# First Y of a delta-rule and MoE kernel placed by products, and the unpacking steps of ScalarE and VectorE given out anew

## The chip, the cores and the metric

One core of a Trainium2 chip runs the whole kernel. The metric is the device time of one execution in microseconds, the median over runs. Engines are called PE (TensorE), PEld (its weight loads), ACT (ScalarE), DVE (VectorE), POOL (GpSimd) and SP (SyncE, which here only starts transfers).

## The reference

```python
# batch 4, 8 heads, 768 steps, head size 48; w_in 384 x 2048, w_out 2048 x 384
for t in range(S):
    y[:, :, t] = einsum('bhd,bhde->bhe', q_t, state)
    v_old = einsum('bhde,bhd->bhe', state, k_t)          # k normalised
    state = state + beta_t * einsum('bhd,bhe->bhde', k_t, v_t - v_old)
x = y.transpose(0, 2, 1, 3).reshape(3072, 384)
h = x @ w_in
g = where(h >= 1, h, where(h <= -1, 0, (h + 1)**2 / 4))
out = g @ w_out
```

## The kernel before

The 768 steps are cut into 12 chunks of 64, and two chunks make a pair G = 0 to 5. A chunk goes through a chain: `gram_k`, `gram_q` (products of keys with keys, and of queries with keys), a triangular solve on DVE in steps of 16-blocks (L312 multiply, L314 subtract), merges of the solved blocks on PE (`merge16_a`, `merge16_b`, `merge32`), `chain_r` and `chain_u` (rows of the state's update, copied from PSUM into the tile SU), `chain_y` (the chunk's Y) and `chain_d` (the new state). `scale_v` and the masks L235 prepare the next operands on DVE, with work of ACT.

Y of a pair is written to XB, in two parts: a rounded one (hi, ACT) and the rest (lo, DVE, L479), so that full-precision products can be made from three fast ones. XB wants the 384 model columns in three groups of 128 rows. A head has 48 columns and a bank row 64, so of every four heads three stand where they belong with the gap between them filled by the fourth, cut in three parts of 16. In all chunks that fourth quarter is first put in a staging tile (`stg`, L477 for its lo part) and then moved by six transfers that SP starts (L482). 

The MoE part runs in items, one weight tile of 128 columns (`f`, 16 of them) and a pair's tokens each. `up` makes nine products (L638), then ACT clamps twice (L777) and squares (L804), DVE takes the maximum (L806), `rest` splits the result into `ghi` (ACT, L772) and `glo` (DVE, L773), and two items later `down` (LAG = 2) adds it into four output banks (L653). The first pair, G = 0, has 22 items: tiles 0 to 5 with the first chunk's tokens only, then tiles 6 to 15 with both chunks', then tiles 0 to 5 with the second chunk's. It is only here that weight tiles are unpacked, each in five steps: grow (ACT, L179), shift (DVE, L181), join (DVE, L183), cast to the hi part (ACT, L187), and low, the lo part (DVE, L189). Four buffers (X4, `xb`) hold tiles in work. Tiles wt11 to wt15 get their weights late, and their rooms serve as scratch before.

Order: the kernel is written under a manual schedule, so every engine works in the order in which the code issues its instructions. `stage` runs the pieces of the front, the part ahead of item 0: products on PE, some steps of ACT and DVE, then their evictions (`finish`). In the items, `at(pe, G, t, ...)` and `at(fill, G, t, ...)` hang pieces on half items: t = 2.5 is the second half of item 2. Before, the generator `unpack` fixed which steps of which tiles go together, as in the following lines, and it was advanced at three places in an item.

```python
        for f in range(2, FT):
            step(f + 1)
            step(f)
            yield
            step(f)
            step(f)
            yield
            step(f - 1)
            yield
```

The idle products, L586 (`IDLE` = 34 of them), stand in the front while the first solve runs on DVE. Chunk names in the text: the first pair holds chunks 0 and 1, the second pair 2 and 3.

Of the kernel before, what the change touches and what calls it, by code (L numbers as in the profile page):

```python
# [27 lines left out]


@with_exitstack  # L30
def delta_rule_moe(ctx: ExitStack, tc: tile.TileContext, kqa, kqb, kv, beta, w, out):
# [142 lines left out]
    def weight(f):  # L174

        x = X4[:, f % 4]
        st = RAW.pop(f)
        sti, xi = st.bitcast(I32), x.bitcast(I32)
        nc.scalar.activation(out=x, in_=st[:, :, 1::2], func=AF.Prelu, scale=2.0 ** -112, alpha=2.0 ** 32)  # L179
        yield  # L180
        nc.vector.tensor_scalar(out=xi, in0=xi, scalar1=3, scalar2=None, op0=ALU.logical_shift_left)  # L181
        yield
        nc.vector.scalar_tensor_tensor(out=xi, in0=sti[:, :, 0::2], scalar=29, in1=xi, op0=ALU.logical_shift_right, op1=ALU.bitwise_or)  # L183
        yield
# [1 line left out]
        hi, lo = (WT[f][:, :, i, :] for i in range(2))
        nc.scalar.copy(out=hi, in_=x)  # L187
        yield
        nc.vector.tensor_tensor(out=lo, in0=x, in1=hi, op=ALU.subtract)  # L189
        yield  # L190
# [231 lines left out]
    def chain_u(g):  # L422
        b_ = banks(D)
        for j in range(H):
            for e, o in quarters():
# [2 lines left out]
                nc.tensor.matmul(b_[t][o * C:o * C + C, j], XT[r, g % 2, k, :], KV[g][r, 1, k, :], start=True, stop=True)  # L428

        def evict():  # L430
            for o in range(2):
                nc.scalar.copy(out=SU[o * C:o * C + C, o, 0:H], in_=b_[1][o * C:o * C + C])  # L432
            nc.scalar.copy(out=SU[:, 0, H:NU], in_=b_[0])
        return evict

    def chain_y(g):
# [10 lines left out]
        def product(i, e, p, o, x, rows, **how):  # L447
            k = e * H + i * NP + p
            u = (x * NU + k) * D
            nc.tensor.matmul(yy[i][o * C:o * C + C, e, p], SF[rows, u:u + C], w_[rows, x, k, :], **how)  # L450
# [79 lines left out]
    def unpack():  # L530

        gens = [weight(f) for f in range(FT)]

        def step(f):
            if f < FT:
                next(gens[f])
        step(0)
        step(1)
        step(0)
        yield  # L540
        step(0)
        step(0)
        yield
        step(2)
        step(1)
        yield
        step(0)
        yield
        step(1)
        step(1)  # L550
        yield
        for f in range(2, FT):
            step(f + 1)
            step(f)
            yield
            step(f)
            step(f)
            yield
            step(f - 1)
            yield  # L560
        step(FT - 1)
        yield

    def stage(pieces, *fill):
# [36 lines left out]
    run(ln[1], 2)
    stage(one_(merge16_b, 0))
    run(ln[1])
    early = solve(), unlanes(1)
    stage(one_(merge32, 0, None, True), (early[0], 4))
    weight_loads(4, 5, nc.scalar)
    stage(one_(merge32, None, 0), (sv[0], 2), (early[0], 4))
    stage(both(chain_u, 0), (raws[0][1], 9), (wu, 2))
    weight_loads(5, 6, nc.scalar)
    stage(both(chain_y, 0), (wu, 2))  # L610
    weight_loads(6, 7)
    stage(both(chain_d, 0), (wu, 2))
    stage(one_(merge16_a, 1), (wu, 2))
# [75 lines left out]
    def plan(G):  # L689

        a, b = 2 * G + 2, 2 * G + 3
        if G == NS - 1:
            return
        va, vb = scale_v(a), scale_v(b)
        if G == 0:
            for j, f in ((0, merge16_b), (0.5, chain_r), (1, lambda g: merge32(g, None, True)), (2, lambda g: merge32(None, g)), (3, chain_u), (4, chain_y), (5, chain_d)):
                at(pe, G, j, lambda f=f: f(1))
            back = restore()
            at(fill, G, 0, (sv[1], 2))
            at(fill, G, 1, (load_k, b), (weight_loads, 7, 9), (load_q, a), (weight_loads, 9, 10), (load_kv, a), (weight_loads, 10, 13))  # L700
            at(fill, G, 1.5, (back, 1))
            at(fill, G, 2.5, (back, 1), (raws[1][1], 9))
            for j, n in enumerate((2, 2, 3)):
                at(fill, G, 3.5 + j, (early[0], n))
            at(fill, G, 6.5, (early[1], 1))
            at(fill, G, 7, (early[1], 9))
            at(fill, G, 4.5, (load_q, b), (weight_loads, 13, 14))
            at(fill, G, 5.5, (load_kv, b), (weight_loads, 14, 15))
            at(fill, G, 8, (load_k, a + 2), (weight_loads, 15, FT))
            for j in range(2):  # L710
                at(fill, G, 6 + j / 2, (va, 1))
                at(fill, G, 11.5 + j / 2, (vb, 1))
            at(pe, G, 6, lambda: gram_q(a))
            at(pe, G, 7, lambda: chain_r(a))
            at(pe, G, 11, lambda: gram_q(b))
            for j, f in ((8, merge16_a), (9.5, merge16_b)):
                for g in range(2):
                    at(pe, G, j + g / 2, lambda f=f, g=g: f(g))
# [60 lines left out]
    late, last, ready = [], None, []  # L779
    for n, item in enumerate(items):  # L780
        at_, c = 2 * n, cols(item[2])
        finish(late)
# [21 lines left out]
        nc.scalar.activation(out=s[:, c], in_=s[:, c], func=AF.Square)  # L804
# [1 line left out]
        nc.vector.tensor_tensor(out=s[:, c], in0=h[:, c], in1=s[:, c], op=ALU.max)  # L806
# [56 lines left out]
```

## Time and profile before

| what | us |
|---|---|
| median of three runs (lowest, highest) | 621.3 (621.08, 621.97) |
| the profiled execution | 622.07 |
| its span, from first to last instruction | 620.2 |
| PE busy | 584.1 (94%) |
| DVE busy | 395.6 (64%) |
| ACT busy | 393.7 (63%) |
| POOL busy | 29.8 (5%) |

The page cuts the span into 40 slices of 15.5 us; each digit is the busy share of a slice in tenths, and PEclk the clock granted to PE, in tenths of full speed:

```profile
PE   8956978799999999999999999999999999999997
...
DVE  5986579783369882469983389963489954323332
ACT  3436676559666659575568647578646576566664
...
PEclk8556597899999999999999999999999999999999
```

The first nine slices, up to 140 us, hold the front and the first pair's items with a weight tile to unpack: there PE has gaps and a lower clock. After it PE is 90% busy or more in each slice to the last.

### The profile page before, as it was taken

The numbers are of one execution on the slowest core, as the hardware profiler recorded it, in microseconds if no ns is written. First come the engines' busy times: TensorE is split into PE (matmuls) and PEld (weight loads), VectorE is DVE, ScalarE is ACT, GpSimd is POOL, SyncE is SP. The second block draws the span as 40 slices with busy tenths as digits, with TensorE's granted clock in tenths as the row PEclk, the third lists the DMA queues.
The fourth block names the chain that finished last, engine by engine and source line by source line (L and its number), as shares of the span: only waits on it lengthen the run. The fifth ranks groups of instructions, "written<-read, shape, count | busy, mean of one in ns | idle before, by whom it ended". The sixth has DMA issues, their size and how long they took to land.

```text
span 620.2 us, 21724 instructions
## 1 busy us (share of the span) xinstructions
PE 584.1 (94%) x9562; PEld 513.4 (83%) x9562; DVE 395.6 (64%) x832; ACT 393.7 (63%) x685; POOL 29.8 (5%) x62
## 2 busy tenths in 40 slices
PE   8956978799999999999999999999999999999997
PEld 7855866687889888888888888888888888889986
DVE  5986579783369882469983389963489954323332
ACT  3436676559666659575568647578646576566664
POOL 5110000010001000010000020000020000000000
PEclk8556597899999999999999999999999999999999
DMA  5663665400124300215210214210225000020001
GB/s 139 196 199 118 199 217 158 144 3 4 42 61 108 83 21 14 53 31 130 82 30 4 71 39 121 65 30 12 61 62 131 4 3 15 8 59 1 0 1 51
DMA packets 32830, 42.96 MB, mean 69 GB/s; under 512 B 7152, under 2 KB 27440, under 8 KB 32736
## 3 DMA queue, kind: packets, MB, share of 16 engines
q1 hardware_dynamic: 31360, 39.14, 22.5%
q10 hardware_dynamic: 1120, 2.36, 1.1%
q8 instruction: 75, 1.23, 0.8%
q14 instruction: 19, 0.16, 0.1%
q0 software_dynamic: 256, 0.08, 0.1%
HBM read 34.47 MB, written 4.72 MB: 63 GB/s over the span
## 4 chain that ended last, share of the span: by engine, by line
PE 68%; ACT 15%; DVE 7%; SPq 4%; DMA 3%; issue 3%; ACTq 0%; DVEq 0%
PE o L653 27%; PE h L638 26%; PE ch L450 3%; ACT s L777 2%; ACT GG L402 2%; ACT XT L404 2%; PE ch L412 2%; SPq L482 2%; DVE xb L183 2%; PE ch L428 1%; PE ch L221 1%; PE ch L494 1%; ACT s L804 1%; ACT XT L397 1%; ACT ghi L772 1%
## 5 line engine op out<-in xcount | busy, mean ns | idle before, releaser
L638 PE MATMUL h<-xb,wt 128*128 128x512 f32 (+1 forms) x918 | 229.5, 396 | 8.0 <-DMA xb<-wt 7.4
L653 PE MATMUL o<-wt,ghi 128*128 128x384 f32 x768 | 202.8, 346 | 0.0
L638 PEld LDWEIGHTS h<-xb,wt 128*128 128x128 f32 x918 | 167.7, 196 | 41.0 <-ACT xb L179 3.9
L806 DVE TENSOR_TENSOR s<-h,s 128x512 f32<-128x512 f32 (+1 forms) x102 | 66.8, 655 | 132.5 <-ACT s L804 132.3
L653 PEld LDWEIGHTS o<-wt,ghi 128*128 128x128 f32 x768 | 138.8, 190 | 7.0
L653 PE MATMUL o<-wt,glo 128*128 128x384 f32 x384 | 130.6, 340 | 0.0
L772 ACT CAST ghi<-s 128x512 fp32r<-128x512 f32 (+1 forms) x102 | 60.8, 596 | 92.2 <-DVE s L806 74.1
L777 ACT ACTIVATE s<-h,half 128x512 f32<-128x512 f32 (+1 forms) x102 | 67.5, 662 | 40.0 <-PE h L638 39.1
L773 DVE TENSOR_TENSOR glo<-s,ghi 128x512 fp32r<-128x512 f32 (+1 forms) x102 | 66.7, 654 | 39.5 <-ACT ghi L772 39.2
L653 PEld LDWEIGHTS o<-wt,glo 128*128 128x128 f32 x384 | 73.0, 190 | 0.2 <-DVE glo L773 0.2
L777 ACT ACTIVATE s<-s,one 128x512 f32<-128x512 f32 (+1 forms) x102 | 71.6, 702 | 2.2
L804 ACT ACTIVATE s<-s 128x512 f32<-128x512 f32 (+1 forms) x102 | 61.9, 607 | 3.2
L323 DVE TENSOR_TENSOR pr<-A 128x30 f32<-128x30 f32 (+14 forms) x120 | 39.3, 328 | 6.2 <-POOL A L294 4.5
L325 DVE TENSOR_TENSOR A<-A,pr 128x30 f32<-128x30 f32 (+14 forms) x120 | 39.9, 332 | 4.4
L187 ACT CAST wt<-xb 128x768 fp32r<-128x768 f32 x16 | 13.3, 832 | 32.0 <-DVE xb L183 32.0
L450 PEld LDWEIGHTS ch<-Q,SU 64*64 64x64 f32 (+1 forms) x1008 | 22.1, 135 | 4.3 <-ACT ghi L772 1.5
L450 PE MATMUL ch<-Q,SU 64*64 64x64 f32 (+1 forms) x1008 | 24.3, 222 | 0.7 <-ACT SU L432 0.7
L235 DVE TENSOR_TENSOR Q<-ch,mask 64x512 f32<-64x512 f32 (+1 forms) x30 | 20.6, 688 | 0.4
L294 POOL TENSOR_SCALAR_AFFINE_SELECT A<-A 128x1024 f32<-128x1024 f32 x4 | 5.1, 1263 | 314.2 <-DMA xb<-X 259.1
L402 ACT ACTIVATE GG<-ch 32x512 f32<-32x512 f32 x22 | 12.9, 588 | 9.8 <-PE ch L390 9.5
L509 DVE TENSOR_TENSOR SU<-ch,SU 48x384 f32<-48x384 f32 (+1 forms) x29 | 16.1, 555 | 0.4
L390 PEld LDWEIGHTS ch<-XT,GG 32*32 32x32 f32 x704 | 13.1, 110 | 3.7 <-issue 3.0
(150 smaller groups left out, 607.2 us busy)
## 6 DMA issues: line engine op xcount, KB each, us to landing
wt<-in_w_dram SPq DMA_DIRECT2D x14, 768.0 KB, 4.9
out_dram<-wx SPq DMA_DIRECT2D x44, 96.0 KB, 2.2
KV<-in_kv_dram SPq DMA_DIRECT2D x36, 96.0 KB, 2.5
KV<-in_kv_dram SPq DMA_DIRECT2D x72, 48.0 KB, 2.4
KV<-in_kv_dram SPq DMA_DIRECT2D x12, 192.0 KB, 2.7
xb<-X SPq DMA_DIRECT2D x60, 32.0 KB, 2.0
K<-in_kqb_dram SPq DMA_DIRECT2D x12, 128.0 KB, 2.7
Q<-in_kqb_dram SPq DMA_DIRECT2D x12, 128.0 KB, 2.8
```

Of the source, the lines that this page charges most:

```text
L235: nc.vector.tensor_tensor(out=a, in0=a if copied else b, in1=mask[r, None, :].broadcast_to([r.stop - r.start, H, C]), op=ALU.mult)
L323: nc.vector.tensor_tensor(out=pr, in0=A[:, 0:n, j:j + 1].broadcast_to([P, n, m]), in1=A[:, j:j + 1, j + 1:32].broadcast_to([P, n, m]), op= ...
L325: nc.vector.tensor_tensor(out=A[:, 0:n, j + 1:32], in0=A[:, 0:n, j + 1:32], in1=pr, op=ALU.add)
L402: nc.scalar.mul(out=GG[r:r + 32, ga, :, 0:32], in_=y1[r:r + 32], mul=-1.0)
L450: nc.tensor.matmul(yy[i][o * C:o * C + C, e, p], SF[rows, u:u + C], w_[rows, x, k, :], **how)
L638: nc.tensor.matmul(h[:, cols(bs)], WT[f][:, 0, x, k * P:(k + 1) * P], XB[G][:, y, k, cols(bs)], start=(n == 0), stop=(n == 8))
L653: nc.tensor.matmul(oacc[G, k], (ghi, glo)[x][:, k * P:(k + 1) * P], WT[f][:, 1, y, :], start=(new and n == 0), stop=(left[G, b] == 0 and n ...
L772: nc.scalar.copy(out=ghi[:, c], in_=s[:, c])
L773: nc.vector.tensor_tensor(out=glo[:, c], in0=s[:, c], in1=ghi[:, c], op=ALU.subtract)
L777: nc.scalar.activation(out=out, in_=in_, func=AF.Relu, bias=bias, scale=scale)
L804: nc.scalar.activation(out=s[:, c], in_=s[:, c], func=AF.Square)
L806: nc.vector.tensor_tensor(out=s[:, c], in0=h[:, c], in1=s[:, c], op=ALU.max)
```

## The change

The first Y. Chunk 0 no longer uses the staging tile and its six transfers. A new zeroed scratch tile SZ (in the room of wt11, cleared by POOL) takes the fourth quarter's columns of U by three DVE copies (L461), at the places where they fall into the gaps. `chain_y(0)` then makes each Y block by two products that add up in PSUM, one of 64 columns from SZ (L486) and one of 48 from SU (L488): 48 products instead of 32, into three banks instead of two. Three ACT casts (L503) and three DVE subtracts (L508) carry them into XB. One copy of U to SU moves from ACT to DVE (L464).

The steps. `weight` and `unpack` give way to five functions and two lists, `acts` (grow, cast) and `vecs` (shift, join, low). Strings of letters give them out: FRONT, two places in each stage, and FILL, six places in each item (A the next of `acts`, D the next of `vecs`, s t v z scale_v, L lanes, m M masks, S solve, U unlanes, B restore, w and W weight loads on SP and ACT, l the next load of keys, queries or values). The second pair's solve, of which eight steps stood in the front, runs wholly in items 3 to 10. PIECES hangs PE's pieces: the second pair's merges stand some 3.5 items later (merge16), and its merge32 and chain 1.5 items later (14 instead of 12.5). IDLE is 25 instead of 34. `merge16_a` of chunk 1 moves from the front into item 0.

In the front, DVE's order from the update of the first chunk to its Y in XB; Q is the masked query tile, `wt11` the staging tile before and SZ now, KV the values. Before:

```order
L314 TENSOR_TENSOR X_602<-X_602,pr_792 128x2x8x8
L235 TENSOR_TENSOR Q_82<-Q_82,mask_165 64x512 x2
L235 TENSOR_TENSOR Q_82<-Q_82,mask_165 128x512
L181 TENSOR_SCALAR xb_180<-xb_180 128x768
L183 SCALAR_TENSOR_TENSOR xb_180<-wt0_110,xb_180 128x768
L181 TENSOR_SCALAR xb_180<-xb_180 128x768
L189 TENSOR_TENSOR wt0_838<-xb_180,wt0_838 128x2x384
L477 TENSOR_TENSOR wt11_846<-o3_847,wt11_846 128x2x64
L477 TENSOR_TENSOR wt11_846<-o0_848,wt11_846 128x2x64
L479 TENSOR_TENSOR xb_845<-o3_847,xb_845 128x2x3x64
L479 TENSOR_TENSOR xb_845<-o0_848,xb_845 128x2x3x64
```

Now (L262 is the masks' line, L193 and L199 shift and join, L283 a step of scale_v):

```order
L262 TENSOR_TENSOR Q_82<-Q_82,mask_165 64x512 x2
L193 TENSOR_SCALAR xb_182<-xb_182 128x768
L199 SCALAR_TENSOR_TENSOR xb_182<-wt0_110,xb_182 128x768
L262 TENSOR_TENSOR Q_82<-Q_82,mask_165 128x512
L283 TENSOR_TENSOR KV_114<-KV_114,N3_441 128x384
L193 TENSOR_SCALAR xb_182<-xb_182 128x768
L461 COPY wt11_180<-o2_776 64x6x16 x2
L461 COPY wt11_180<-h_775 128x6x16
L464 COPY SU_175<-h_775 128x384
L199 SCALAR_TENSOR_TENSOR xb_182<-wt1_112,xb_182 128x768
L283 TENSOR_TENSOR KV_125<-KV_125,N3_441 128x384
L508 TENSOR_TENSOR xb_823<-o3_824,xb_823 128x2x3x64
```

The solve steps ahead of the masks are gone, the masks and joins stand among others, and the copies into SZ and SU are new.

On ACT in items 0 and 1, with the casts' place after the second clamp and Square. Before:

```order
L777 ACTIVATE s_1022<-s_1022,one_171 128x256
L804 ACTIVATE s_1022<-s_1022 128x256
L187 CAST wt4_1139<-xb_180 128x2x384
L772 CAST ghi_1143<-s_1022 128x256
L777 ACTIVATE s_1157<-h_1147,half_169 128x256
L402 ACTIVATE GG_176<-o3_1159 32x16x32 x2
L179 ACTIVATE xb_180<-wt6_898 128x768
L777 ACTIVATE s_1157<-s_1157,one_171 128x256
L804 ACTIVATE s_1157<-s_1157 128x256
L187 CAST wt5_1242<-xb_180 128x2x384
```

Now (L795 the clamps, L827 Square, L203 the cast, L187 grow, L790 ghi):

```order
L795 ACTIVATE s_939<-s_939,one_171 128x256
L827 ACTIVATE s_939<-s_939 128x256
L203 CAST wt2_1046<-xb_182 128x2x384
L187 ACTIVATE xb_182<-wt5_815 128x768
L203 CAST wt3_1049<-xb_182 128x2x384
L187 ACTIVATE xb_182<-wt6_821 128x768
L790 CAST ghi_1056<-s_939 128x256
L795 ACTIVATE s_1071<-h_1061,half_169 128x256
L203 CAST wt4_1139<-xb_182 128x2x384
L795 ACTIVATE s_1071<-s_1071,one_171 128x256
```

Before, the casts behind the Squares of items 0 and 1 are those of tiles 4 and 5; now they are those of tiles 2 and 3, and of tile 4 in item 1.

On PE around the up of tile 13. Before, the products between the ups of tiles 12 and 13 are the down of tile 10 and the first products of merge32 (L390), with merge16 and the q gram done:

```order
L653 MATMUL o3_1839<-wt10_1659,ghi_2123 128x384 x2
L653 MATMUL o3_1839<-wt10_1659,glo_2124 128x384
L390 MATMUL ch_2230<-XT_177,GG_176 32x32 x32
L638 MATMUL h_2274<-xb_845,wt13_2015 128x512 x9
L390 MATMUL ch_2286<-XT_177,GG_176 32x32
```

Now (L400 is merge16_b, L248 gram_q, L675 up, L690 down):

```order
L400 MATMUL ch_2054<-A16_1952,XT_177 32x16 x64
L675 MATMUL h_2126<-xb_823,wt13_1845 128x512 x9
L690 MATMUL o0_1210<-wt11_1712,ghi_1958 128x384 x2
L690 MATMUL o0_1210<-wt11_1712,glo_1959 128x384
L690 MATMUL o1_1214<-wt11_1712,ghi_1958 128x384 x2
L690 MATMUL o1_1214<-wt11_1712,glo_1959 128x384
L690 MATMUL o2_1677<-wt11_1712,ghi_1958 128x384 x2
L690 MATMUL o2_1677<-wt11_1712,glo_1959 128x384
L690 MATMUL o3_1681<-wt11_1712,ghi_1958 128x384 x2
L690 MATMUL o3_1681<-wt11_1712,glo_1959 128x384
L400 MATMUL ch_2160<-A16_1952,XT_177 32x16 x64
L248 MATMUL ch_2225<-Q_1790,K_1196 64x64 x2
```

The second half of merge16_b, the q gram of chunk 3 and merge32 now stand behind the up of tile 13.

The core of the diff:

```diff
-IDLE = 34
+IDLE = 25
+FRONT = (
+    "AL,L", ",WA", "sL,Amm", "DDmsD,", ",WAADw", "t,", "AtDDD,A")
...
+MERGE = 28
+PIECES = ((0, "a1"), (1, "r1"), (2, "b1"), (4, "c1"), (5, "e1"), (6, "u1"), (8, "y1"), (11, "d1"), (16, "q2"), (19, "r2"), (23, "a2"), (24, "a3"), (25, "b2"), (27, "b3 q3"))
...
+    SZ = room(FT - 5, 0, 2 * CT * 2 * 3 * C).rearrange("p (x i k c) -> p x i k c", x=2, k=3, c=C)
+    nc.gpsimd.memset(SZ, 0.0)
...
         def evict():
-            for o in range(2):
-                nc.scalar.copy(out=SU[o * C:o * C + C, o, 0:H], in_=b_[1][o * C:o * C + C])
-            nc.scalar.copy(out=SU[:, 0, H:NU], in_=b_[0])
+            moves = [(slice(o * C, o * C + C), o, 0, b_[1]) for o in range(2)] + [(slice(0, P), 0, 1, b_[0])]
+            for r, x, e, b in moves:
+                if g == 0:
+                    nc.vector.tensor_copy(out=SZ[r, x, e * CT:e * CT + CT, :, D:C],
+                                          in_=b[r].rearrange("p (i q) (k t) -> p i q k t", q=NP, k=3)[:, :, NP - 1])
+            for r, x, e, b in moves:
+                (nc.vector.tensor_copy if g == 0 and e else nc.scalar.copy)(out=SU[r, x, e * H:e * H + H], in_=b[r])
...
+        def placed(i, e, p, o, x, rows):
+            k = e * H + i * NP
+            y = yy[i] if i == 0 or e else y0
+            nc.tensor.matmul(y[o * C:o * C + C, e, p], SZ[rows, x, e * CT + i, p], w_[rows, x, k + 3, :], start=True, stop=False)
+            u = (x * NU + k + p) * D
+            nc.tensor.matmul(y[o * C:o * C + D, e, p], SF[rows, u:u + D], w_[rows, x, k + p, :], start=False, stop=True)
+
+        if g == 0:
+            y0 = ps.tile([P, CT, NP, C], F32, **acc())
+            for i in range(NT):
+                for p in range(3):
+                    for e in range(2):
+                        for o in range(2):
+                            r = o if (e, i) != (1, 1) else 1 - o
+                            placed(i, e, p, o, (o, 0)[e], slice(r * C, r * C + C))
...
+    def stage(pieces, n):
         evicts = products(*pieces)
-        for gen, m in fill:
-            run(gen, m)
+        codes = FRONT[n].split(",")
+        do(codes[0])
         finish(evicts)
+        do(codes[1])
...
+    acts = [(f, grow) for f in range(2)] + [x for f in range(FT) for x in ((f + 2, grow), (f, cast)) if x[0] < FT]
+    vecs = [x for f in range(FT + 1) for x in ((f, shift), (f, join), (f - 1, low)) if 0 <= x[0] < FT]
...
-            M = 12.5
+            M = MERGE / 2
...
-            t, n = (-2.5, 19) if G == 1 else (-1.5, 17)
+            t, n = (MERGE / 2 + 7 - FT - HALF, 31 + 2 * HALF - MERGE) if G == 1 else (-1.5, 17)
```

More of the change, by code (lines that the diff above doesn't have):

```diff
@@ L170, in delta_rule_moe, with grow @@
     nc.gpsimd.memset(SF, 0.0)
+    SZ = room(FT - 5, 0, 2 * CT * 2 * 3 * C).rearrange("p (x i k c) -> p x i k c", x=2, k=3, c=C)
+    nc.gpsimd.memset(SZ, 0.0)
     X4 = sb.tile([P, 4, 2, DM], F32, name="xb")
[L174 to L184, printed above, removed]
-        WT[f] = const.tile([P, 2, 2, DM], F32R, name=f"wt{f}")
[L186 to L190, printed above, removed]
+    def grow(f):
+        X = X4[:, f % 4]
+        if PRELU:
+            nc.scalar.activation(out=X, in_=RAW[f][:, :, 1::2], func=AF.Prelu, scale=2.0 ** -112, alpha=2.0 ** 32)
+        else:
+            nc.scalar.mul(out=X, in_=RAW[f][:, :, 1::2], mul=2.0 ** -112)
@@ new lines, in shift, with join @@
+    def shift(f):
+        x = X4[:, f % 4].bitcast(I32)
+        nc.vector.tensor_scalar(out=x, in0=x, scalar1=3, scalar2=None, op0=ALU.logical_shift_left)
+    def join(f):
+        x = X4[:, f % 4].bitcast(I32)
+        if not PRELU:
+            nc.vector.scalar_tensor_tensor(out=x, in0=RAW[f].bitcast(I32)[:, :, 1::2], scalar=-0x80000000, in1=x, op0=ALU.bitwise_and, op1=ALU.bitwise_or)
+        nc.vector.scalar_tensor_tensor(out=x, in0=RAW.pop(f).bitcast(I32)[:, :, 0::2], scalar=29, in1=x, op0=ALU.logical_shift_right, op1=ALU.bitwise_or)
@@ new lines, in cast, with low, unpack @@
+    def cast(f):
+        WT[f] = const.tile([P, 2, 2, DM], F32R, name=f"wt{f}")
+        nc.scalar.copy(out=WT[f][:, :, 0, :], in_=X4[:, f % 4])
+    def low(f):
+        nc.vector.tensor_tensor(out=WT[f][:, :, 1, :], in0=X4[:, f % 4], in1=WT[f][:, :, 0, :], op=ALU.subtract)
+    done = set()
+    def unpack(steps):
+        for f, x in steps:
+            for g, y in ((f, dict(zip(UNPACK[1:], UNPACK)).get(x)), (f - 4, low if x is grow else None)):
+                assert y is None or g < 0 or (g, y) in done, (f, x)
+            x(f)
+            done.add((f, x))
+            yield
@@ L193, in quarters @@
+    UNPACK = grow, shift, join, cast, low
     def quarters():
@@ L439, in chain_y @@
             XB[g // 2] = sb.tile([P, 2, 3, 2 * NB], F32R, name="xb")
-        if g < 2:
-            stg = const.tile([P, 2, 2 * DM], F32R, name=f"wt{(FT - 5, FT - 1)[g]}")[:, :, 0:NB]
-        else:
+        if g == 1:
+            stg = const.tile([P, 2, 2 * DM], F32R, name=f"wt{FT - 1}")[:, :, 0:NB]
+        elif g > 1:
             stg = sb.tile([P, 2, NB], F32R, name="X", bufs=1)
@@ L450, in product, with direct, after @@
             nc.tensor.matmul(yy[i][o * C:o * C + C, e, p], SF[rows, u:u + C], w_[rows, x, k, :], **how)
+        def placed(i, e, p, o, x, rows):
[12 more added lines that the diff above has]
+                            placed(i, e, p, o, (o, 0)[e], slice(r * C, r * C + C))
+            def direct():
+                parts = []
+                for y, i, es in ((yy[0], 0, slice(0, 2)), (y0, 1, slice(0, 1)), (yy[1], 1, slice(1, 2))):
+                    hi, lo = (xb[:, x, :, 0:NB].rearrange("p k (e s t) -> p s e k t", s=CT, t=C)[:, i, es] for x in range(2))
+                    nc.scalar.copy(out=hi, in_=y[:, es, 0:3])
+                    parts.append((y[:, es, 0:3], hi, lo))
+                def after():
+                    for y, hi, lo in parts:
+                        nc.vector.tensor_tensor(out=lo, in0=y, in1=hi, op=ALU.subtract)
+                return after
+            return direct
         for i in range(NT):
@@ L528, in run @@
                 break
[L530 to L564, printed above, removed]
+    def stage(pieces, n):
         evicts = products(*pieces)
-        for gen, m in fill:
-            run(gen, m)
+        codes = FRONT[n].split(",")
+        do(codes[0])
         finish(evicts)
+        do(codes[1])
     def restore():
@@ L575, in delta_rule_moe, with do @@
     spare += START
-    wu, sv, ln, raws = unpack(), [scale_v(0), scale_v(1)], [lanes(0), lanes(1)], []
+    acts = [(f, grow) for f in range(2)] + [x for f in range(FT) for x in ((f + 2, grow), (f, cast)) if x[0] < FT]
+    vecs = [x for f in range(FT + 1) for x in ((f, shift), (f, join), (f - 1, low)) if 0 <= x[0] < FT]
+    sv, ln, raws = [scale_v(g) for g in range(4)], [lanes(0), lanes(1)], []
+    tasks = {"A": unpack(acts), "D": unpack(vecs), "B": restore(), "L": ln[1], "s": sv[0], "t": sv[1], "v": sv[2], "z": sv[3]}
+    loads = [(load_k, 3), (load_q, 2), (load_kv, 2), (load_q, 3), (load_kv, 3), (load_k, 4)]
+    tile_ = [4]
+    def do(codes):
+        for c in codes:
+            if c in "wW":
+                weight_loads(tile_[0], tile_[0] + 1, nc.scalar if c == "W" else nc.sync)
+                tile_[0] += 1
+            elif c == "l":
+                f, g = loads.pop(0)
+                f(g)
+            else:
+                run(tasks[c], 1)
     for g in range(2):
@@ L598, in delta_rule_moe @@
     one_ = lambda f, *a: [lambda: f(*a)]
-    stage(one_(merge16_a, 0))
     place_beta(1, NS)()
[L601 to L613, printed above, removed]
+    stage(one_(merge16_a, 0), 0)
+    stage(one_(merge16_b, 0), 1)
+    tasks.update({"m": raws[0][1], "M": raws[1][1], "S": solve(), "U": unlanes(1)})
+    stage(one_(merge32, 0, None, True), 2)
+    stage(one_(merge32, None, 0), 3)
+    stage(both(chain_u, 0), 4)
+    stage(both(chain_y, 0), 5)
+    stage(both(chain_d, 0), 6)
     spare[:] = START[0:2] + START[4:6]
@@ L693, in plan @@
             return
-        va, vb = scale_v(a), scale_v(b)
         if G == 0:
[L696 to L718, printed above, removed]
-            M = 12.5
+            made = dict(a=lambda g: merge16_a(g % 2), b=lambda g: merge16_b(g % 2), c=lambda g: merge32(g, None, True), e=lambda g: merge32(None, g), u=chain_u, y=chain_y, d=chain_d, r=chain_r, q=gram_q)
+            for j, names in PIECES:
+                for x in names.split():
+                    at(pe, 0, j / 2, lambda f=made[x[0]], g=int(x[1]): f(g))
+            M = MERGE / 2
             last = FT + HALF
@@ L781, in delta_rule_moe @@
         at_, c = 2 * n, cols(item[2])
+        codes = FILL[n].split(",") if n < len(FILL) else [""] * 6
+        do(codes[0])
         finish(late)
+        do(codes[1])
         if last:
@@ L785, in delta_rule_moe @@
             ready.append(last[0])
+        do(codes[2])
         if at_ == 2 * HALF:
             spare.clear()
+        assert (item[1], low) in done, item
         h = up(*item)
@@ L792, in delta_rule_moe @@
         evicts = products(*pe.pop(at_, []))
-        run(wu, 3 if n == 0 else 1)
+        do(codes[3])
         fills(at_)
         finish(evicts)
-        run(wu, 1)
+        do(codes[4])
         if len(ready) == LAG:
@@ L806, in delta_rule_moe @@
         nc.vector.tensor_tensor(out=s[:, c], in0=h[:, c], in1=s[:, c], op=ALU.max)
-        run(wu, 1)
+        do(codes[5])
         fills(at_ + 1)
```

5 lines of the change are left out of this document (added).

## The prediction

> **What bounds the kernel now.** I read the page's slices first, then busy time by stretches (us, then busy us and count of PE, PEld, DVE, ACT and POOL, granted clock, DMA share, GB/s), cut where the first MoE item, item 13 and the second pair's items begin.
>
> ```profile
> core 0: us, PE busy (x) PEld busy (x) DVE busy (x) ACT busy (x) POOL busy (x), PEclk, DMA share, GB/s
> ...
> 29.00:60.69 31.69, 19.43 (x723) 17.34 (x727) 24.04 (x55) 13.05 (x26) 1.99 (x3) 0.55 0.47 146
> 60.69:141.84 81.15, 70.17 (x1517) 61.26 (x1517) 61.95 (x110) 52.05 (x90) 3.65 (x7) 0.82 0.46 144
> 141.84:191.47 49.63, 46.92 (x1002) 41.78 (x998) 26.09 (x62) 36.00 (x74) 3.50 (x6) 0.97 0.17 43
> 191.47:600.00 408.53, 406.61 (x5772) 355.13 (x5772) 257.61 (x544) 270.50 (x460) 10.52 (x18) 1.00 0.18 46
> ```
>
> From 191.47 on PE is busy 406.61 of 408.53 us at full clock and the change leaves those items alone: whatever is won must be won ahead of 191.47, and it counts only as an earlier start of that stretch. From 141.84 to 191.47 PE is nearly the bound too (46.92 of 49.63). So I ask when item 13 starts, and what is moved behind it.
>
> The front next: the timeline (start, length, idle before in brackets), with the last transfer taken from the chain of waits.
>
> ```profile
> 43.06 2.12 DVE L235 TENSOR_TENSOR Q<-Q,mask 64x512 f32<-64x512 f32 x3
> ...
> 45.69 0.96 DVE L183 SCALAR_TENSOR_TENSOR xb<-wt,xb 128x768 int32<-128x768 int32 x1
> ...
> 46.73 0.83 ACT L187 CAST wt<-xb 128x768 fp32r<-128x768 f32 x1 [3.28 <-DVE xb L183]
> 47.59 0.97 ACT L432 COPY SU<-o 64x384 f32<-64x384 f32 x2
> 48.12 3.53 PE L450 MATMUL o<-Q,SU 112*64 112x64 f32 x64 [4.33 <-ACT SU L432]
> ...
> 53.12 1.01 DVE L479 TENSOR_TENSOR xb<-o,xb 128x384 fp32r<-128x384 f32 x2
> 54.20 3.96 SPq L482 DMA_DIRECT2D xb<-wt  x6
> ...
> 59.67 0.98 PE L638 MATMUL h<-xb,wt 128*128 128x256 f32 x3 [0.23 <-DMA xb<-wt]
> 60.69 0.47 ACT L777 ACTIVATE s<-h,half 128x256 f32<-128x256 f32 x1 [1.27 <-PE h L638]
> ```
>
> ```profile
> 57.56 1.97 DMA xb<-wt
> ```
>
> Two things stand between the state update of the first chunk and item 0. ACT stands 3.28 us in the weight cast L187, which waits for the join L183, which waits for three masks on DVE; the copy of U to SU is queued behind it, so PE idles 4.33 us ahead of the first Y. And after the last subtract of Y (54.13) six transfers of the fourth quarter take to 59.53.
>
> The items up to 11: first and last maximum, the busy time between them, and who waited (total us, times, longest).
>
> ```profile
> 64.36 0.42 DVE L806 TENSOR_TENSOR s<-h,s 128x256 f32<-128x256 f32 x1 [0.17 <-ACT s L804]
> ...
> 138.00 0.69 DVE L806 TENSOR_TENSOR s<-h,s 128x512 f32<-128x512 f32 x1
> ```
>
> ```profile
> 64.36:138.00 73.64, 63.30 (x1272) 55.00 (x1273) 57.11 (x101) 46.22 (x80) 2.61 (x5) 0.83 0.49 152
> ```
>
> ```profile
> ACT wt L187 <- DVE xb L183: 26.1, 12, 4.8
> DVE glo L773 <- ACT ghi L772: 8.5, 8, 2.2
> DVE s L806 <- ACT s L804: 8.2, 6, 3.1
> ```
>
> No engine is full here: DVE has 57.11 of 73.64 (77.6%), its other 16.5 us are the 8.5 + 8.2 of waits on ACT, and ACT in turn stands 26.1 us in twelve casts that wait for DVE's join just issued. It is a ping-pong of two in-order queues, and items 0 to 11 go at its pace.
>
> **Part 1: first Y by products.** It removes the staging subtracts, six transfers and their wait (54.13 to 59.53, 5.4 us) and it frees SP's queue of 3.96 us of issue; no other transfer stands close behind on SP there, so I cost that at nothing. The U copies now come ahead of the cast on ACT, and the third copy and three small ones of the fourth quarter run on DVE. The end of the update's products, near 43.8, I leave: it hangs on DVE's solve steps and merges. For the IDLE products (25 instead of 34) I count nothing: they end at 29.00, 2.0 later than they would, but the transposes that the first merge needs end at 28.95 (row below), so DVE is the cover. Nor for the new clear of SZ: POOL does it while the first keys are still on their way.
>
> ```profile
> 27.94 1.01 DVE L350 STREAM_TRANSPOSE XT<-A 128x512 f32<-128x512 f32 x1
> ```
>
> ```profile
> 36.83 0.19 DVE L312 TENSOR_TENSOR pr<-X,A 128x30 f32<-128x30 f32 x1
> ...
> 42.85 0.29 DVE L314 TENSOR_TENSOR X<-X,pr 128x128 f32<-128x128 f32 x1
> ```
>
> ```profile
> 21.54 7.46 PE L586 MATMUL o<-SU 128*64 128x32 f32 x68
> ```
>
> ```profile
> L428 PE MATMUL o<-KV,XT x32: 303/303/338, 41.8 to 43.5; 64*64 64x48 f32 x32
> ```
>
> Two copies of U take 0.97 on ACT; with the four on DVE beside them the copies end 1.2 to 1.6 us after 43.8, and Y starts near 45.2 (before 48.12). Y is 48 products, 96 passes, instead of 64 passes. Bounds: 32 passes of each of two banks of the update, 64 in all, took 41.8 to 43.8, 31 ns each, so 3.0 us; the idle products, all on one place of the array, 7.46/68 = 110 ns, so 10.5 us. Nearest is the old Y itself, same operands and two alternating places: 3.53/64 = 55 ns, so 5.3. I take 5.3, ending at 50.5 against 51.65. Behind it a cast and subtracts (about 1, from the 1.01 row), a KV step (0.55) and the low part of tile 0 (0.95, both rows below) stand before the last three products (0.98): relu of item 0 at 54.1, not 60.69. Its maximum comes 2.2 later (three ACT steps of 0.47 and a copy), at 56.3 instead of 64.36, because the casts that stood in between come elsewhere. The lead here is 8.1.
>
> The Trainium skill speaks against this part ("TensorE: Matmul & The Clock Gate", Part 3, The mechanism): a weight load is pulled ahead of running products only if its row group doesn't conflict, and each new pair uses the same rows twice running. No run yet shows the new sequence; by that rule the 110 ns apply, which is the second rival.
>
> **Part 2: items 0 to 11.**
>
> ```profile
> L189 DVE TENSOR_TENSOR wt<-xb,wt 128x768 fp32r<-128x768 f32 x12 | 11.4, 951 | 0.0
> L183 DVE SCALAR_TENSOR_TENSOR xb<-wt,xb 128x768 int32<-128x768 int32 x12 | 11.4, 948 | 0.0
> L181 DVE TENSOR_SCALAR xb<-xb 128x768 int32<-128x768 int32 x12 | 6.6, 546 | 0.0
> ...
> ```
>
> ```profile
> L256 DVE TENSOR_TENSOR KV<-KV,N 128x384 f32<-128x384 f32 x2 | 1.1, 552 | 0.0
> ```
>
> ```profile
> 135.52 2.11 DVE L235 TENSOR_TENSOR Q<-ch,mask 64x512 f32<-64x512 f32 x3
> ```
>
> ```profile
> 130.00 0.71 DVE L379 STREAM_TRANSPOSE GG<-XT 128x512 f32<-128x512 f32 x1
> ```
>
> DVE's work between the two maxima: 57.1; plus eight solve steps that stood in the front, at 0.19 + 0.29 = 0.48 each, 3.8; plus one weight tile, 0.95 + 0.95 + 0.55 = 2.45; less a set of masks that comes later, 2.1; less one merge's transpose, 0.7: 60.6. What goes is the cast's wait, since a cast now stands a step or more behind its join. DVE's own idle time, 16.5 over 12 items or 1.4 each, was mostly the echo of that; a round trip from Square to the maximum remains. Bounds: all of it stays (16.5) or none (0). Walking the two new queues side by side with these durations leaves about half, 0.75 an item, 9 us. So 60.6 + 9 = 69.6, DVE 87% busy, the last maximum at 125.9 (138.00 before). Item 13 then starts near 126.9: it came 3.84 after that maximum since tile 13's low part was late, and I take 1.0 without that. Lead 14.9.
>
> Weight loads are issued in another order on SP and ACT; with a DMA share of 0.46 in this stretch I count nothing for them. The cover is the lead of two tiles in unpacking.
>
> **Part 3: what is moved behind item 13.** Half the second pair's merge16_b, its q gram and half its merge32 (PE's groups from 60.69 to 141.84: busy us, mean ns; the first two rows hold both halves or both grams, the third one the half that moves):
>
> ```profile
> L373 PE MATMUL ch<-A,XT 32*32 32x16 f32 x256 | 2.9, 180 | 0.7 <-issue 0.7
> ...
> L221 PE MATMUL ch<-Q,K 48*64 48x64 f32 x128 | 2.7, 242 | 0.0
> ...
> L390 PE MATMUL ch<-XT,GG 32*32 32x32 f32 x64 | 1.2, 192 | 0.0
> ...
> ```
>
> ```profile
> 177.13 2.28 PE L450 MATMUL ch<-Q,SU 112*64 112x64 f32 x96
> ...
> 180.50 1.23 PE L638 MATMUL h<-xb,wt 128*128 128x256 f32 x9
> ```
>
> ```profile
> 183.40 4.65 SPq L482 DMA_DIRECT2D xb<-X  x6
> ```
>
> 2.9/2 + 2.7/2 + 1.2 = 4.0 us of PE work that was done while PE had room is now paid where it has none. Next, the Y of chunk 3 comes 1.5 items later. From it to the landing of its six transfers is 183.40 + 4.65 + 1.97 - 177.13 = 12.9 us, and PE had 14.3 of work (to 191.47). Without 1.5 items of an up (1.23) and a down about as long, 3.6, 10.7 are left: a new stall of about 2.1 before the second pair's first item. DVE's steps pushed back cost an estimated 1 more there. Bounds for these two: 0 to 5 (the 1.27 ahead of the first relu is the like). Together 7.1.
>
> **Sum.** 14.9 - 7.1 = 7.8 off 622.07 (the profiled execution; span 620.2) is 614.3; the median of the runs is 0.77 lower, so 613.5 on its basis. The likeliest case's own range, from 2 us either way on the 9 of idle time and on the 3.1 of stall: 609.5 to 617.5.
>
> **Rivals.**
> *Two queues part fully* (R3). DVE stops waiting and PE's own work sets the pace: 63.30 us from 56.3, item 13 at 120.6, lead 21.2, net 14.1: 607.2. For it: 26.1 us of ACT's waits go. Against it: the clock.
>
> ```profile
> 60.00:70.00 10.00, 9.30 (x270) 8.50 (x270) 7.45 (x15) 5.60 (x10) 1.04 (x2) 0.50 0.40 121
> 70.00:80.00 10.00, 10.00 (x155) 9.44 (x155) 3.66 (x7) 7.83 (x14) 0.31 (x1) 0.54 0.90 303
> ```
>
> With PE busy 9.30 and 10.00 of 10 the granted clock stayed at 0.50 and 0.54. The Trainium skill ("TensorE: Matmul & The Clock Gate", Part 1, What's actually happening) says that one busy window of some 3.4 us opens the clock; here the trace differs (20 us near half speed), so I give that way little. By it a denser start would land on R3's figure.
>
> *Placed products run singly* (R2). 96 passes at 110 ns, 10.6 instead of 5.3: 5.3 later everywhere, net 2.5, 618.8. For it: each pair stays on one place. Against it: the old Y's 55 ns with repeated places at its start.
>
> *The share of DVE stays* (R1, slower). A new ping-pong takes the cast's place: Square waits behind unpacking casts on ACT, the maximum behind joins on DVE, whose queue has grown to 60.6. At 77.6% that is 78.1, the last maximum at 134.4, item 13 at 137.7 with its low part late as now, lead 4.1, less 7.1: 3.0 slower, 624.3. It decides where the lead equals 7.1, that is at a share of about 79.5% (76 us). For it: both queues stay in order and both have more work per time. Against it: ACT has only 46.22 of 73.64.
>
> **How the numbers follow.** Forecast 0.52, R3 0.20, R2 0.12, R1 0.12, no visible change 0.04. The forecast, R3 and most of R2 are faster: 0.82; same 0.05 (0.03 of that last case and some of R2); slower 0.13. I call 0.2% (1.2 us) the least that can be told apart. The range 605 to 620 holds the first three cases, R3 with 2 us to spare, R2 with 1, and leaves out R1 and the rest.
>
> **What would show it.** Right: Y's products start near 45 and last about 5, no transfer before item 0, its relu near 54; casts no longer wait on joins; DVE above 85% between the maxima of items 0 and 11; item 13 near 127; a stall near 2 us just ahead of the second pair's first item, which starts near 184. Wrong: Y's products above 8 us, the DVE share under 80%, or a stall above 5 there.

## The result, and the profile after

| | before | changed |
|---|---|---|
| median of the runs, us | 621.2 | 611.41 (609.53 to 612.58) |
| the profiled execution, us | 622.07 | 611.8 |
| its span, us | 620.2 | 610.1 |
| granted clock, mean | 0.935 | 0.948 |

The ratio to the kernel before is 0.9837 (95% interval 0.9810 to 0.9864): faster by 1.6%, where 613.5 was forecast within 605 to 620.

The same cuts as before, at the relu of item 0, the up of item 13 and the first up of the second pair (columns as above: us, busy us of PE, PEld, DVE, ACT, POOL, clock, DMA share, GB/s):

```profile
core 0: us, PE busy (x) PEld busy (x) DVE busy (x) ACT busy (x) POOL busy (x), PEclk, DMA share, GB/s
...
29.00:55.77 26.77, 17.35 (x630) 15.73 (x632) 18.39 (x39) 12.29 (x22) 2.36 (x3) 0.57 0.60 211
55.77:125.77 70.00, 63.00 (x1389) 54.92 (x1387) 62.85 (x121) 51.56 (x89) 1.57 (x3) 0.88 0.45 145
125.77:179.46 53.69, 50.83 (x1261) 44.57 (x1254) 28.64 (x62) 37.92 (x78) 4.62 (x9) 0.97 0.15 38
179.46:588.00 408.54, 405.51 (x5765) 353.79 (x5766) 259.38 (x552) 268.72 (x457) 11.51 (x20) 1.00 0.18 47
```

The lead is 4.9 us at item 0's relu (55.77 against 60.69), 16.1 at item 13 (125.77 against 141.84), 12.0 at the second pair (179.46 against 191.47) and 10.1 at the end. The items gave 11.2 us (70.00 for 81.15), the stretch behind item 13 took 4.1 back (53.69 for 49.63), in which PE is busy 50.83 instead of 46.92.

Between the maxima of items 0 and 11, and who waited there (total, times, longest):

```profile
58.29:124.36 66.07, 59.85 (x1106) 52.16 (x1105) 58.95 (x117) 48.50 (x82) 1.57 (x3) 0.87 0.46 150
```

```profile
ACT wt L203 <- DVE xb L199: 5.5, 2, 5.1
...
DVE s L829 <- ACT s L827: 4.2, 3, 2.6
...
DVE glo L791 <- ACT ghi L790: 0.7, 2, 0.5
```

The kernel before, between the same two maxima (64.36 to 138.00):

```profile
ACT wt L187 <- DVE xb L183: 22.6, 11, 4.8
```

DVE is busy 58.95 of 66.07, 89% (78% before). ACT's waits in casts for joins fell from 22.6 to 5.5 us. (The 26.1 of the prediction are those of the longer stretch from 60.69 to 141.84; the changed kernel has 6.9 between its own two cuts.)

The front did not do what was forecast. ACT's and PE's rows there:

```profile
42.79 0.89 ACT L187 ACTIVATE xb<-wt 128x768 f32<-128x768 f32 x1 [4.23 <-DMA wt<-in_w_dram]
43.71 1.18 ACT L424 COPY XT<-h 32x512 f32<-32x512 f32 x2
...
44.98 0.34 PE L455 MATMUL o<-KV,XT 64*64 64x48 f32 x2 [4.46 <-ACT XT L424]
...
47.27 0.47 PE L486 MATMUL o<-Q,wt 64*64 64x64 f32 x2 [0.33 <-DVE wt L461]
```

The grow of weight tile 2 stands 4.23 us on ACT for its tile to land, and two copies that the state update reads (L424) are queued behind it. The update's products start at 44.98, where the old kernel had them from 41.8.

Behind the last cut 1.9 us of lead are lost, 12.0 to 10.1. Two waits on PE, which the kernel before doesn't have at these places, make 1.3 of them:

```profile
188.84 0.44 PE L690 MATMUL o<-wt,glo 128*128 128x384 f32 x1 [0.40 <-DVE glo L791]
...
220.64 1.20 PE L417 MATMUL ch<-XT,GG 32*32 32x32 f32 x64 [0.91 <-DVE XT L360]
```

The second is merge32 of the third pair, waiting for DVE's solve, whose steps were pushed back with the second pair's chain. It has 0.87 to 0.91 us in nine of the ten profiles with this order of the merges (the tenth has 1.77 in the first wait instead), 0.21 where merge32 and the chain stand half an item earlier (MERGE = 27, below), and none in the two with the old order.

### The profile page after: what moved, and what is told of

Same layout as the page of the kernel before. It is cut to its first block, busy times and chain, and to the rows that moved or that the text cites. A ratio compares the mean times of both kernels' runs of the same rounds, so it can differ in the third digit from the quotient of the medians.

```text
span 610.1 us, 21744 instructions
## 1 busy us (share of the span) xinstructions
PE 577.8 (95%) x9576; PEld 506.4 (83%) x9576; DVE 395.8 (65%) x835; ACT 393.2 (64%) x683; POOL 31.9 (5%) x63
## 4 chain that ended last, share of the span: by engine, by line
PE 68%; ACT 10%; SPq 6%; DVE 6%; DMA 6%; issue 2%; DVEq 0%; ACTq 0%
PE h L675 27%; PE o L690 27%; DMA wt<-in_w_dram 3%; PE ch L481 3%; ACT GG L429 2%; ACT s L795 2%; ACT XT L431 2%; PE ch L439 2%; PE ch L248 2%; PE ch L455 1%; PE ch L417 1%; PE ch L554 1%; PE ch L419 1%; ACT s L827 1%; DMA Q<-in_kqb_dram 1%
## 5 line engine op out<-in xcount | busy, mean ns | idle before, releaser
L675 PE MATMUL h<-xb,wt 128*128 128x512 f32 (+1 forms) x918 | 228.6, 393 | 4.6 <-DMA xb<-wt 2.3
L690 PE MATMUL o<-wt,ghi 128*128 128x384 f32 x768 | 200.7, 343 | 0.0
L675 PEld LDWEIGHTS h<-xb,wt 128*128 128x128 f32 x918 | 165.5, 193 | 38.8 <-issue 2.4
L690 PEld LDWEIGHTS o<-wt,ghi 128*128 128x128 f32 x768 | 137.7, 189 | 7.1
L690 PE MATMUL o<-wt,glo 128*128 128x384 f32 x384 | 130.0, 339 | 1.9 <-DVE glo L791 1.9
L790 ACT CAST ghi<-s 128x512 fp32r<-128x512 f32 (+1 forms) x102 | 60.8, 596 | 102.0 <-DVE s L829 93.1
L795 ACT ACTIVATE s<-h,half 128x512 f32<-128x512 f32 (+1 forms) x102 | 67.6, 663 | 38.9 <-PE h L675 38.1
L690 PEld LDWEIGHTS o<-wt,glo 128*128 128x128 f32 x384 | 72.4, 189 | 2.8 <-DVE glo L791 2.8
L795 ACT ACTIVATE s<-s,one 128x512 f32<-128x512 f32 (+1 forms) x102 | 71.7, 702 | 2.3
L827 ACT ACTIVATE s<-s 128x512 f32<-128x512 f32 (+1 forms) x102 | 61.9, 607 | 3.2
L481 PEld LDWEIGHTS ch<-Q,SU 64*64 64x64 f32 (+3 forms) x1056 | 22.5, 135 | 4.5 <-ACT ghi L790 1.5
L481 PE MATMUL ch<-Q,SU 64*64 64x64 f32 (+3 forms) x1056 | 24.7, 222 | 0.7 <-ACT SU L464 0.7
L262 DVE TENSOR_TENSOR Q<-ch,mask 64x512 f32<-64x512 f32 (+1 forms) x30 | 20.6, 687 | 0.9 <-PE ch L248 0.4
L187 ACT ACTIVATE xb<-wt 128x768 f32<-128x768 f32 x16 | 14.5, 905 | 8.9 <-DMA KV<-in_kv_dram 4.7
L417 PEld LDWEIGHTS ch<-XT,GG 32*32 32x32 f32 x768 | 14.9, 113 | 6.3 <-issue 4.2
L417 PE MATMUL ch<-XT,GG 32*32 32x32 f32 x768 | 16.4, 200 | 2.7 <-issue 1.0
```

What stands on the lines that cost most here:

```text
L417: nc.tensor.matmul(y1[r:r + 32, u], GG[r + 32:r + 64, ga, u, 0:32], XT[r + 32:r + 64, ga, u, 32:64], start=True, stop=True)
L675: nc.tensor.matmul(h[:, cols(bs)], WT[f][:, 0, x, k * P:(k + 1) * P], XB[G][:, y, k, cols(bs)], start=(n == 0), stop=(n == 8))
L690: nc.tensor.matmul(oacc[G, k], (ghi, glo)[x][:, k * P:(k + 1) * P], WT[f][:, 1, y, :], start=(new and n == 0), stop=(left[G, b] == 0 and n ...
L790: nc.scalar.copy(out=ghi[:, c], in_=s[:, c])
L795: nc.scalar.activation(out=out, in_=in_, func=AF.Relu, bias=bias, scale=scale)
```

## The experiments

**The first Y in the old way, all steps in the new.** Edit:

```diff
 chain_u(0): U copied by ACT alone, no copies into SZ
 chain_y(0):
-    placed(...), direct()
+    stg in the room of wt11, 32 products, two staging subtracts, six transfers
```

> The changed kernel with the first Y as before: staging tile, two staging subtracts and six transfers, 32 products, U copied by ACT alone; all steps stay given out as in the changed kernel. Theory (the front's lead is the Y's, and the items carry it to the end): the state update's products stay near 45, but relu of item 0 comes some 5.5 us later than 55.8 (transfers and landing 5.4), and since DVE sets the items' pace the delay is carried: 616.5 (615.5 to 617.5). Rival (items wait for unpacking anyway, and absorb a late item 0): under 613.

Measured: 619.1 us, ratio 0.9951 (0.9930 to 0.9972). The first maximum comes at 63.96 instead of 58.29, 5.7 later as the theory has it; the time is 7.7 longer, more than either said. The ten runs spread from 615.7 to 620.9, so some lie in the theory's range and the profiled one (619.86) does not.

```profile
ACT s L793 <- PE h L673: 4.2, 1, 4.2
```

```profile
63.96:130.79 66.83, 61.86 (x1092) 53.61 (x1084) 59.06 (x115) 48.37 (x82) 1.57 (x3) 0.83 0.46 149
```

While the transfers run, ACT stands 4.2 us for item 0: its casts are now given out behind that. The delay is carried, and not absorbed, through items at a slightly lower clock (0.83): the maximum of item 11 comes 6.4 later than in the changed kernel.

**The first Y by products, all steps in the old way.** Edit:

```diff
 the kernel before
+    SZ, its memset, its three copies; one U copy on DVE
+    chain_y(0) by placed(...) and direct()
```

> The kernel before with only the first Y by products (SZ, three small copies, one U copy on DVE, 48 products, no staging, no transfers); steps, merges and IDLE as before. Theory: Y starts near 48 as before, since U's copies still stand behind the cast that waits for its join; it lasts 5, and relu of item 0 comes near 56 instead of 60.7; carried through: 616.5 (615.5 to 618). Rival (the ping-pong of casts and joins absorbs it): 620 to 621.

Measured: 620.0 us, ratio 0.9974 (0.9958 to 0.9990). The rival was right, at its lower end. ACT from the casts of Y to item 0's first clamp (L812):

```profile
53.42 0.54 ACT L478 CAST xb<-o 128x192 fp32r<-128x192 f32 x2 [0.80 <-PE o L463]
55.35 0.83 ACT L189 CAST wt<-xb 128x768 fp32r<-128x768 f32 x1 [1.39 <-DVE xb L185]
56.09 0.91 ACT L181 ACTIVATE xb<-wt 128x768 f32<-128x768 f32 x1
56.90 1.46 ACT L539 COPY SU<-ch 48x384 f32<-48x384 f32 x3
58.25 0.83 ACT L189 CAST wt<-xb 128x768 fp32r<-128x768 f32 x1
58.99 0.38 ACT L368 COPY wt<-h 128x256 f32<-128x256 f32 x1
59.25 0.49 ACT L812 ACTIVATE s<-h,half 128x256 f32<-128x256 f32 x1
```

Item 0's first product starts at 56.19 and its clamp only at 59.25, 1.4 earlier than before: the unpacking that had lain under the transfers now lies bare ahead of it. So by medians the Y alone gives 1.5 us, the steps alone 2.4 (621.51 less 619.1), and both together 9.8. Most of what is more than the sum arises ahead of item 0: its first maximum comes 0.4 earlier than before with the steps alone (63.96), 1.4 with the Y alone (62.94) and 6.1 with both (58.29). With the Y alone the unpacking takes its place, as above. With the steps alone Y starts at 48.26, no earlier than before (48.12), since tile 2's landing holds the update there too (43.44), and the six transfers still follow. That this is all of it was not tested.

**A cast at each join again.** Edit:

```diff
 def join(f):
     ...
+    cast(f)
 acts: (f, cast) becomes a step that does nothing
```

> The changed kernel, but each weight tile's cast stands in ACT's order where its join is issued, not where the table puts it; the other steps stay where they are. Theory (the casts that stand apart made the items faster): ACT again waits 20 us or more in casts for joins, DVE's share between the maxima of items 0 and 11 falls from 88% to about 80%, item 13 comes 6 to 9 us later than 125.8, and the time is 618 to 620. Rival (the items gain by the moved solve, merges and earlier loads, and the casts' waits were cover for nothing): 611 to 613, with the waits back all the same.

Measured: 624.1 us, ratio 1.0042 (1.0020 to 1.0064): slower than the kernel before, and 12.7 slower than the changed one, which is beyond the 618 to 620 of the theory.

```profile
60.50:135.01 74.51, 62.91 (x1106) 52.97 (x1105) 59.44 (x115) 48.16 (x81) 1.57 (x3) 0.87 0.43 138
```

```profile
ACT wt L208 <- DVE xb L199: 19.1, 11, 5.9
```

DVE has the same work (59.44 against 58.95) in 74.51 us, 80%. ACT's waits are back at 19.1 us. Nothing but the casts' place differs, so it is shown that this place is what made the items faster. Of the 12.7, 8.4 are lost in this stretch, 2.2 ahead of it (first maximum) and 2.1 behind it.

**Tile 2's grow behind the copies.** Edit:

```diff
-"sL,Amm", "DDmsD,"
+"sL,mm", "DDmsD,A"
```

> The changed kernel with one step moved: the grow of weight tile 2, which on ACT stands ahead of two copies that the state update needs and waits 4.23 us for the tile's landing (42.79), now stands behind them. Theory (that wait cost the front the 2.9 us by which the update starts later than before, 44.95 against 41.8): update's products near 42, item 0 some 2.9 earlier, carried: 608.5 (607.8 to 609.5). Rival (the tiles' landing and DVE's queue hold items 0 to 3 anyway): 611 as it is.

Measured: 608.39 us, ratio 0.9787 (0.9756 to 0.9817), as the theory had it.

```profile
41.03 1.18 ACT L424 COPY XT<-h 32x512 f32<-32x512 f32 x2 [2.00 <-PE h L419]
42.70 0.90 ACT L187 ACTIVATE xb<-wt 128x768 f32<-128x768 f32 x1 [0.48 <-DMA wt<-in_w_dram]
```

The copies run at 41.03, 2.7 earlier, and wait for PE alone. The first maximum comes 2.3 earlier (55.96).

**Y's products ordered by rows.** Within each half of Y, each product has its predecessor's rows. Edit:

```diff
+for half in range(2):
     for i in range(NT):
         for p in range(3):
             for e in range(2):
-                for o in range(2):
-                    r = o if (e, i) != (1, 1) else 1 - o
-                    placed(i, e, p, o, (o, 0)[e], slice(r * C, r * C + C))
+                o = half if (e, i) != (1, 1) else 1 - half
+                placed(i, e, p, o, (o, 0)[e], slice(half * C, half * C + C))
```

> The changed kernel with the 48 products of the first Y in another order: first all 24 that use rows 0 to 63 of the array, then all 24 of rows 64 to 127, so that each product has the rows of the one before it. Theory (the price of a product comes from its rows being in use: 110 ns a pass on one place, 35 to 55 when two places alternate): 96 passes take 8 to 10.5 us instead of the 3.6 us measured from 48.64 to 52.27, and item 0 comes 5 to 7 us later. Rival (the idle products' 110 ns had another reason, and a pass costs 35 to 40 ns here too): Y takes 3.5 to 4 as it does, item 0 unmoved.

Measured: 610.78 us in one run. Y's rows (two passes, and four passes, per row):

```profile
47.32 0.42 PE L486 MATMUL o<-Q,wt 64*64 64x64 f32 x2
47.53 0.42 PE L488 MATMUL o<-Q,SU 64*48 64x64 f32 x2
...
```

```profile
49.45 0.48 PE L486 MATMUL o<-Q,wt 64*64 64x64 f32 x4
49.66 0.48 PE L488 MATMUL o<-Q,SU 64*48 64x64 f32 x4
```

Rows of two passes start 0.21 apart: 107 ns a pass, as the idle products (110). These are products on one place, rows and columns alike. The rows of four passes, also 0.21 apart, belong to the blocks whose columns alternate between two halves of the array: 54 ns, with the same rows. The granted clock is 0.50 over all of these rows. So the theory was right that a place in use has its price, and wrong that the rows alone make it. The changed order shows the same at the same clock: its first 24 products alternate between two places (rows and columns both) and start 53 ns a pass apart (49.23 to 50.94), its last 24 go round four places and start about 28 ns apart (50.94 to 51.71).

Y lasts 8.3 us (46.20 to 54.53) where the changed order takes 5.1 (47.27 to 52.33), and its first maximum is late (61.89). Yet by item 3 the maximum comes at 79.78 against 80.04, and the time is no longer: the theory was wrong on what follows. The clock, in the last section, goes with this.

**Idle products back to 34.** Edit:

```diff
-IDLE = 25
+IDLE = 34
```

> The changed kernel with 34 idle products again. Theory (the solve and its transposes end last, the idle products are cover): merge16_a starts as now within 0.3 us, time 611.4 within 1.2. Rival (the cut freed the front): merge16_a 1 to 2 us later, time 612.5 to 613.5.

Measured: 609.63 us, ratio 0.9809 (0.9788 to 0.9829): no loss, and 0.6 below the theory's range. merge16_a starts at 29.27 against 28.98, as the theory had it. In this profile tile 2 landed by 40.73 rather than 42.79.

**Chunk 3's q gram earlier.** Edit, with the grow moved:

```diff
-(23, "a2"), (24, "a3"), (25, "b2"), (27, "b3 q3")
+(22, "q3"), (23, "a2"), (24, "a3"), (25, "b2"), (27, "b3")
```

> The kernel with tile 2's grow behind the copies, and besides chunk 3's q gram back ahead of item 12, where the old kernel had it. Theory (PE work behind item 13 is paid in full, ahead of it there is room): 1.0 to 1.35 less than with the grow moved alone (608.4), about 607.2. Rival (PE is 91% busy ahead of item 13 too, so the gram is paid there as well): 608.4 as it is.

Measured: 616.91 us, ratio 0.9916 (0.9895 to 0.9938). Both were wrong: it costs 8.5.

```profile
PE ch L386 <- DVE Q L262: 9.8, 1, 9.8
```

The gram's result holds its PSUM bank until DVE has masked it. DVE is busy without a gap there, from 111.7 to 125, and comes to the masks only at 121.78, 10.5 us after the gram; merge16_a, the next to want a bank, stands 9.8 us on PE. The price was a bank, not PE time.

**merge32 and the chain half an item earlier.** Edit, with the grow moved:

```diff
-MERGE = 28
+MERGE = 27
```

> The kernel with tile 2's grow behind the copies, and the second pair's merge32 and chain half an item earlier (27 instead of 28 half items). Theory (no stall is left ahead of the second pair's first item, 0.63 us at most, so an earlier chain has nothing to win): 608.4 within 1. Rival (the late Y of chunk 3 still holds the first items of the second pair): 606.5 to 607.4.

Measured: 611.91 us, ratio 0.9837 (0.9817 to 0.9856), 3.5 more than with the grow moved alone. Neither range holds this.

```profile
133.72 1.92 PE L417 MATMUL ch<-XT,GG 32*32 32x32 f32 x64 [1.56 <-DVE Q L262]
```

merge32 now waits 1.56 us for the masks, ahead of a DVE that stands 6.5 and 4.5 us for ACT a little later (at most 4.6 and 3.6 with the grow moved alone). That an earlier chain won nothing agrees with the theory, that it cost something doesn't; how the 3.5 divides between this and the clock (0.87 and 0.95 in the two stretches, against 0.92 and 1.00) stays open.

**On one chip: the changed kernel, the grow moved as above, and IDLE = 34 besides.** No other edit.

> The changed kernel as it is, as the base of the next two on the same chip. 611.4 within 0.8; by the theory that tile 2's landing sets the start of the update (40.7 to 43.4 in the profiles so far), tile 2's grow ends a wait and the copies start at its end, wherever the landing falls in this profile.

> The kernel with tile 2's grow behind the copies, once more beside the changed kernel. Theory (the wait for the landing is taken off the front): 1.5 to 3 less than the changed kernel on the same chip, copies for the update at 40.5 to 41.5. Rival (the first 608.4 was the clock's luck, its items ran at 0.92 instead of 0.87): within 1 of the changed kernel.

> The same with 34 idle products. Theory (609.6 with 34 idle products came of an early landing, 40.73 against 42.79): with the landing off the path no difference from the grow moved alone, within 0.7. Rival (the idle products hold the clock up, and 34 are worth 1 to 2 us): 1 to 2 less.

Measured: 611.88 (ratio 0.9833, 0.9808 to 0.9858), 609.30 (0.9805, 0.9776 to 0.9835) and 610.82 (0.9815, 0.9787 to 0.9844). In the changed kernel's second profile tile 2's grow ends a wait of 4.02 us for the landing (43.39) and the copies follow at 44.30, as the theory had it. The moved grow is lower both times, by 3.0 and 2.6, with intervals that still overlap: the best version seen, by some 2 to 3 us. With 34 idle products the first merge came 2.5 later in the profile, against the theory. First the kernel with 34, then with 25:

```profile
22.76 7.46 PE L629 MATMUL o<-SU 128*64 128x32 f32 x68
30.98 1.91 PE L386 MATMUL o<-XT,GG 32*32 32x16 f32 x128
```

```profile
21.41 5.54 PE L629 MATMUL o<-SU 128*64 128x32 f32 x50
28.48 1.90 PE L386 MATMUL o<-XT,GG 32*32 32x16 f32 x128 [0.69 <-DVE XT L375]
```

The idle products start at 20.73 to 22.76 in the profiles, after the keys' products. When that is early, DVE's transposes end last and their number is free (idle34, 21.05); when it is late, 34 of them end last, here 2.5 us later than the other profile's merge. The difference of the medians (1.5) is within the intervals.

## Why the prediction was right

Point by point, by its own steps:

- *The items* were right in mechanism, and their size was underrated. 69.6 us were forecast between the maxima, 4.0 less than before; it was 66.07, 7.6 less. Work was 58.95 instead of 60.6, DVE's idle time 7.1 instead of 9: a share of 89%, not 87%. The 26.1 us of ACT's waits that the prediction shows for this stretch are those of a longer one; between the maxima it was 22.6. The run with casts at the joins shows the mechanism.
- *The slower rival* (R1) is what that run resembles: a share of 80%, item 13 at 137.2 where 137.7 was worked out, 624.1 us where 624.3 was. The prediction's sum for it has slips: with the 3.84 us "as now" item 13 comes at 138.2 and the time is 624.8, and the share at which it decides is about 81%, not 79.5%. The closeness of the times is partly luck, for the first maximum was at 60.50 and not at 56.3.
- *The moved PE work* was right: 4.0 forecast; PE is busy 3.9 longer behind item 13.
- *The stall of 2.1 and DVE's 1 more* ahead of the second pair failed as to their place: PE waits 0.63 us there and the whole stretch is 4.06 longer, which the moved work alone fills. Part is paid later: 1.9 of lead goes behind the cut (12.0 to 10.1), of which 1.3 are the two waits for DVE shown above. So the loss behind item 13 was 6.0 in all, where 7.1 was forecast.
- *"The end of the update's products, near 43.8, I leave"* failed. It followed DVE's steps and the idle products, and left out a DMA wait on ACT that the new order put ahead of the copies. The update came 3.2 later, and Y 2.1 later (47.27 for 45.2). The run with the grow moved shows that this wait is the cause: there the copies come 2.7 earlier. So item 0's lead was 4.9 where 6.6 was forecast and the first maximum's 6.1 instead of 8.1.
- *Y's price* was right in its sum, 5.3 forecast and 5.1 measured, but not as a constant 55 ns a pass.

```profile
48.64:52.27 3.63, 3.63 (x103) 3.63 (x107) 1.46 (x3) 2.08 (x3) 0.00 (x0) 0.56 0.70 221
```

Ninety of the 96 passes have records in this stretch, 40 ns each on the average of two halves: 53 ns on two places, about 28 on four, the last half microsecond at a higher clock. The second rival (110 ns) fell. The Trainium skill's sentence in "TensorE: Matmul & The Clock Gate", Part 3, The mechanism, which has a weight load overlap only when the row group differs, holds in part: products on one place cost 107 ns in the run ordered by rows. But those with the same rows and other columns cost 54 there, no more than those that change rows too (53).
- *The idle products at nothing* was right for the execution it was read from; in a later pair of profiles the first merge came 2.5 us later with 34 of them.

The misses partly cancel, in us of lead: the first maximum 2.0 short, the items between the maxima 3.5 better, the step from there to item 13 0.4 short, the loss behind it 1.1 less. Together, with rounding, the lead at the end was 10.1 where 7.8 was forecast. That the sum came out 2.1 from the median owes something to luck.

## What to carry to other kernels

Put a step that only feeds another engine's later work at some distance from the step that it reads from: two in-order queues that hand each other one buffer in turn both stand, though neither is full. A removed wait pays only if the work that lay under it has another place, and a moved step must be checked for every wait it brings to its queue, landings of transfers and holds on PSUM banks among them. One edit's gain can depend on the other: 1.5 and 2.4 apart were 9.8 together.
